# A linear-attention and GEGLU kernel on one core: the first v cast without Pool, one PSUM copy on ScalarE, and the last 128 output rows in three column parts

## The chip, the cores and the metric

One core of a Trainium2 chip. The metric is the device time of one execution in microseconds (us); smaller is better. A traced execution also has a span, from its first to its last instruction, some 1.8 us shorter than the time.

Engines in the profile: PE is TensorE's matmuls, PEld its weight loads, DVE is VectorE, ACT is ScalarE, POOL is GpSimd (Pool in the text), SP issues most transfers.

## The reference

```python
q_s = softmax over the last axis of q          # (8, 8, 576, 64)
k_s = softmax over the sequence axis of k
kv  = einsum('bhsd,bhse->bhde', k_s, v)
x   = einsum('bhsd,bhde->bhse', q_s, kv)       # transposed to (4608, 512)
out = (gelu(x @ w_gate) * (x @ w_val)) @ w_out # d_ff 1536, out (4608, 512) float32
```

## The kernel before

Everything runs in fp16 on TensorE. Per batch: exponentials of q and k, a cast of v, transposes of q (`unit_t`), the products of k and v (`unit_kv`), x transposed (`unit_x`), then the feed-forward stage (`ffn_fi`, 12 slices) and the output matmuls (`mm_out`), of which each row block of 128 ends in one PSUM bank and is evacuated (copied to SBUF) and stored by `evac`. Names in the profile: `eqt` is the transposed softmax of q, copied out of the PSUM tile `pst`; `pskv` holds the products of k and v, `kv_sb` what is kept of them; `xt` is x transposed, copied out of `psx`; `psg` and `psv` are the gate and value products, `ht` the input of the output matmuls. The parts that matter here (cut, `...` where lines are left out):

```python
ps_big = tile_pool(bufs=6, space=PSUM)     # six banks, tag "mm"
ps_att = tile_pool(bufs=2, space=PSUM)     # two banks, tag "att"

def unit_kv(b, g):
    pskv = ps_att.tile([P, 2, 2 * VW], f32, tag="att")
    # ... 2 x 5 matmuls, then VectorE: a reciprocal (rck) and two kv_sb ...

def unit_t(b, g, eng="dve"):
    pst = ps_att.tile([P, 2, MAIN], f16, tag="att")
    # ... 8 transposes ...
    copy_on(eng, eqt[:, 2 * g:2 * g + 2, 0:MAIN], pst)

# in evac, for the last row block of all (psy is one bank, hc = 256)
nc.vector.tensor_scalar(out=yo[:, 0:hc], in0=psy[:, 0:hc], ...)
store(nc.sync, yo[:, 0:hc], ns, ns + 1, 0, hc)
nc.scalar.activation(out=yb, in_=psy[:, hc:C], func=ACTF.Copy, ...)
store(nc.scalar, yb, ns, ns + 1, hc, C)

# the first batch, in program order
unit_t(0, 0, "dve")
warm_pe(6)                      # six matmuls that keep TensorE busy
cast_v(0, 0, 4, "dve")          # heads 0 to 3
cast_v(0, 4, 6, "act")
unit_t(0, 1, "dve")
cast_v(0, 6, 8, "pool")
unit_kv(0, 0); unit_kv(0, 1)
unit_x(0, 0, "act", True); unit_x(0, 1, "act", True)
cast_w("wg", 0, "pool"); cast_w("wv", 0, "pool")
unit_x(0, 2, "dve", True); unit_x(0, 3, "dve", True)
```

The softmax here doesn't subtract the row's maximum and nothing guards it: scores larger than these inputs give would overflow.

## Time and profile before

| | before |
|---|---|
| time, median of the first three runs | 329.2 us (329.01 to 329.72) |
| traced span | 327.7 us |
| PE busy | 317.5 us, 97% |
| first value matmul (all earlier work is ramp) | 18.88 us |
| last matmul's end to the end of the span | 323.53 to 327.7 us, 4.2 us |

How to read it: only where the chain of waits leaves PE can a microsecond be gained, which is at the two ends. The lines of the busy shares, of the chain and of both ends are in the prediction. One more pair of lines will matter, which I did not look at before predicting: the timeline of the kernel before near 73 us (start, duration in us, engine, line, operation, output<-inputs, shapes, count, and in brackets the idle time before it with its releaser).

```profile
73.18 0.82 DVE L167 TENSOR_TENSOR eq<-eq,rrq 128x640 f16<-128x640 f16 x1
73.22 2.69 POOL L119 CAST v<-vt 128x640 f16<-128x640 f32 x3 [10.70 <-PE psg L268]
```

VectorE's normalization (two SBUF inputs) starts 0.04 us ahead of Pool's v casts and takes 0.82 us.

### The profile page before, as it was taken

The numbers are of one execution on the slowest core, as the hardware profiler recorded it, in microseconds if no ns is written. First come the engines' busy times: TensorE is split into PE (matmuls) and PEld (weight loads), VectorE is DVE, ScalarE is ACT, GpSimd is POOL, SyncE is SP. The second block draws the span as 40 slices with busy tenths as digits, with TensorE's granted clock in tenths as the row PEclk, the third lists the DMA queues.
The fourth block names the chain that finished last, engine by engine and source line by source line (L and its number), as shares of the span: only waits on it lengthen the run. The fifth ranks groups of instructions, "written<-read, shape, count | busy, mean of one in ns | idle before, by whom it ended". The sixth has DMA issues, their size and how long they took to land.

```text
span 327.7 us, 4481 instructions
## 1 busy us (share of the span) xinstructions
PE 317.5 (97%) x1702; PEld 153.1 (47%) x1702; DVE 180.5 (55%) x327; ACT 146.0 (45%) x195; POOL 46.4 (14%) x59
## 2 busy tenths in 40 slices
PE   7699999999999999999999999999999999999994
PEld 2444454445454544554455445444544444444441
DVE  2753365497579636952597349733983233333331
ACT  3453574898344572349224922484243033103300
POOL 1576452303002100030004000300000000000000
PEclk9599999999999999999999999999999999999999
DMA  7999999960196016900590039202100110040002
GB/s 229 363 384 392 402 393 389 392 248 0 64 315 233 3 64 208 338 1 23 176 393 19 2 132 380 99 0 86 45 0 2 64 64 2 4 108 19 1 33 96
DMA packets 38358, 50.49 MB, mean 154 GB/s; under 512 B 2112, under 2 KB 34112, under 8 KB 38336
## 3 DMA queue, kind: packets, MB, share of 16 engines
q1 hardware_dynamic: 38192, 50.08, 42.9%
q8 instruction: 13, 0.21, 0.2%
q10 hardware_dynamic: 144, 0.13, 0.1%
q14 instruction: 9, 0.07, 0.1%
HBM read 40.76 MB, written 9.44 MB: 153 GB/s over the span
## 4 chain that ended last, share of the span: by engine, by line
PE 89%; DMA 5%; ACT 2%; DVE 2%; issue 1%; SPq 1%; POOL 0%; POOLq 0%; ACTq 0%
PE psy L312 28%; PE psv L268 26%; PE psg L268 26%; DMA kt<-in_k_dram 3%; PE pskv L194 3%; PE pst L219 2%; PE psx L246 2%; DMA qt<-in_q_dram 1%; PE pswarm L260 1%; SPq L103 1%; ACT xt L121 1%; DVE kv_sb L202 0%; PE pstr L231 0%; DVE rq L160 0%; ACT L143 0%
## 5 line engine op out<-in xcount | busy, mean ns | idle before, releaser
L273 ACT ACTIVATE gl<-psg 128x512 f32<-128x512 f32 x108 | 63.9, 598 | 137.9 <-PE psg L268 131.5
L275 DVE SCALAR_TENSOR_TENSOR ht<-psv,gl 128x512 f16<-128x512 f32 x108 | 73.9, 689 | 65.3 <-PE psv L268 63.2
L268 PE MATMUL psg<-xt,wg_sb 128*128 128x512 f16 x384 | 100.6, 379 | 0.7 <-ACT xt L121 0.5
L268 PE MATMUL psv<-xt,wv_sb 128*128 128x512 f16 x384 | 100.2, 379 | 0.1
L312 PE MATMUL psy<-wo_sb,ht 128*128 128x512 f16 x432 | 95.8, 379 | 0.0
L268 PEld LDWEIGHTS <-wv_sb 128*128 128x128 f16 x432 | 42.3, 98 | 51.8 <-issue 1.3
L312 PEld LDWEIGHTS <-ht 128*128 128x128 f16 x432 | 41.6, 98 | 48.5
L268 PEld LDWEIGHTS <-wg_sb 128*128 128x128 f16 x432 | 41.0, 98 | 44.8 <-issue 1.6
L346 DVE TENSOR_SCALAR yo<-psy 128x512 f32<-128x512 f32 x31 | 21.2, 687 | 49.2 <-PE psy L312 49.2
L119 POOL CAST v<-vt 128x640 f16<-128x640 f32 x26 | 20.6, 830 | 141.5 <-PE psx L246 64.3
L160 DVE TENSOR_REDUCE rq<-eq 128x10 f32<-128x640 f16 (+1 forms) x32 | 25.3, 791 | 10.2 <-ACT eq L143 10.2
L167 DVE TENSOR_TENSOR eq<-eq,rrq 128x640 f16<-128x640 f16 (+1 forms) x27 | 23.1, 856 | 0.9
L121 ACT CAST xt<-psx 128x512 f16<-128x512 f32 x26 | 14.5, 587 | 18.5 <-PE psx L246 18.5
L143 ACT ACTIVATE eq<-qt 128x2560 f16<-128x2560 f32 (+1 forms) x9 | 18.3, 2049 | 4.4 <-DMA qt<-in_q_dram 4.3
L143 ACT ACTIVATE ek<-kt 128x2048 f16<-128x2048 f32 (+1 forms) x10 | 15.6, 1558 | 4.2 <-DMA kt<-in_k_dram 4.2
L219 PE MATMUL pst<-ident,eq 128*128 128x128 f16 x128 | 10.7, 228 | 3.6 <-DVE eq L167 2.0
L219 PEld LDWEIGHTS <-eq 128*128 128x128 f16 x128 | 8.9, 102 | 7.9 <-ACT eq L143 2.5
L194 PEld LDWEIGHTS <-ek 128*128 128x128 f16 x160 | 11.0, 101 | 3.1
L268 PE MATMUL psg<-xtr,wg_sb 128*128 128x512 f16 x48 | 12.3, 379 | 0.0
L268 PE MATMUL psv<-xtr,wv_sb 128*128 128x512 f16 x48 | 12.3, 379 | 0.0
L194 PE MATMUL pskv<-v,ek 128*128 128x130 f16 x160 | 12.3, 227 | 0.0
L123 DVE COPY eqt<-pst 128x1024 f16<-128x1024 f16 x16 | 10.9, 679 | 0.6 <-PE pst L219 0.6
(52 smaller groups left out, 132.1 us busy)
## 6 DMA issues: line engine op xcount, KB each, us to landing
kt<-in_k_dram SPq DMA_DIRECT2D x14, 640.0 KB, 7.6
vt<-in_v_dram SPq DMA_DIRECT2D x14, 640.0 KB, 9.0
qt<-in_q_dram SPq DMA_DIRECT2D x14, 640.0 KB, 6.2
out_dram<-yo SPq DMA_DIRECT2D x14, 512.0 KB, 3.0
wost<-in_moe_w_out_dram SPq DMA_DIRECT2D x6, 512.0 KB, 8.8
wgst<-in_moe_w_gate_dram SPq DMA_DIRECT2D x5, 512.0 KB, 7.4
wvst<-in_moe_w_val_dram SPq DMA_DIRECT2D x5, 512.0 KB, 7.9
kt<-in_k_dram SPq DMA_DIRECT2D x4, 320.0 KB, 8.7
```

The costliest lines, as they stand in the source:

```text
L119: nc.gpsimd.tensor_copy(out=dst, in_=src)
L121: nc.scalar.copy(out=dst, in_=src)
L143: nc.scalar.activation(out=dst[:, c0:c1, h0 * D:h1 * D].rearrange("p n (h d) -> p h n d", d=D), in_=tiles[(nm, b)][:, h0:h1, c0 * D:c1 * D ...
L160: nc.vector.reduce_sum(rq, e, axis=mybir.AxisListType.X)
L167: (nc.gpsimd if eng == "pool" else nc.vector).tensor_tensor(out=e, in0=e, in1=rrq.unsqueeze(-1).to_broadcast((P, n, 2, D)), op=ALU.mult)
L194: nc.tensor.matmul(pskv[:, j, :], ek_b[b % 2][:, n, hp * P:(hp + 1) * P], v16_b[b % 2][:, n, 2 * hp:2 * hp + 2, 0:VW], start=(n == 0), sto ...
L219: nc.tensor.transpose(pst[:, j, n * P:(n + 1) * P], eq_b[b % 2][:, n + 1, hp * P:(hp + 1) * P], ident)
L268: nc.tensor.matmul(ps, w[:, ci, fi * P:(fi + 1) * P], xt[:, ci, :], start=(ci == 0), stop=(ci == HP - 1))
L273: nc.scalar.activation(out=gl, in_=psg, func=ACTF.Gelu)
L275: nc.vector.scalar_tensor_tensor(out=ht, in0=psv, scalar=_H_SCALE, in1=gl, op0=ALU.mult, op1=ALU.mult)
L312: nc.tensor.matmul(psy, hts[fi][:, ns * P:(ns + 1) * P], wo_sb[:, fi, :], start=(fi == 0), stop=(fi == NFI - 1))
L346: nc.vector.tensor_scalar(out=yo, in0=psy, scalar1=1.0 / _H_SCALE, scalar2=None, op0=ALU.mult)
```

## The change

Its intent at the start is to take Pool out of the first batch's v cast and a copy off VectorE; at the end, to have less work left when the last matmul ends.

```diff
-    htp = ctx.enter_context(tc.tile_pool(name="htp", bufs=14))
+    htp = ctx.enter_context(tc.tile_pool(name="htp", bufs=13))
...
+    def last_rows(b, hts, ns):
+        cuts = ((0, 256), (256, 384), (384, 512))
+        ps = [ps_big.tile([P, c1 - c0], f32, name="psl", tag="mm") for c0, c1 in cuts]
+        for part in ((0,), (1, 2)):
+            for fi in range(NFI):
+                for i in part:
+                    c0, c1 = cuts[i]
+                    nc.tensor.matmul(ps[i], hts[fi][:, ns * P:(ns + 1) * P], wo_sb[:, fi, c0:c1],
+                                     start=(fi == 0), stop=(fi == NFI - 1))
+            for i in part:
+                c0, c1 = cuts[i]
+                yl = yop.tile([P, c1 - c0], f32, name=f"yl{i}", tag=f"yl{i}", bufs=1)
+                if i < 2:
+                    nc.vector.tensor_scalar(out=yl, in0=ps[i], scalar1=1.0 / _H_SCALE,
+                                            scalar2=None, op0=ALU.mult)
+                else:
+                    nc.scalar.activation(out=yl, in_=ps[i], func=ACTF.Copy, scale=1.0 / _H_SCALE)
+                store(nc.scalar if i == 2 else nc.sync, yl, b, ns, ns + 1, c0, c1)
...   (the old two-halves code in evac goes; store is the same, moved out of evac)
-    unit_t(0, 1, "dve")
-    cast_v(0, 6, 8, "pool")
+    unit_t(0, 1, "act")
+    cast_v(0, 6, 8, "dve")
     unit_kv(0, 0)
     unit_kv(0, 1)
+    cast_w("wg", 0, "pool")
+    cast_w("wv", 0, "pool")
     unit_x(0, 0, "act", True)
     unit_x(0, 1, "act", True)
-    cast_w("wg", 0, "pool")
-    cast_w("wv", 0, "pool")
     unit_x(0, 2, "dve", True)
-    unit_x(0, 3, "dve", True)
+    unit_x(0, 3, "act", True)
```

More of the change, by code (lines that the diff above doesn't have):

```diff
@@ L313, in mm_out, with out_rows, store @@
                              start=(fi == 0), stop=(fi == NFI - 1))
+    def out_rows(b):
+        return out[b * S:(b + 1) * S, :].rearrange("(m n) c -> m n c", n=NT)
+    def store(eng, src, b, n0, n1, c0=0, c1=C):
+        base = out_rows(b)[:, 1 + n0:1 + n1, c0:c1]
+        (pm, nm), (pn, _), _ = base.ap
+        last = [[1, (n1 - n0) * C]] if c1 - c0 == C else [[1, c1 - c0]]
+        eng.dma_start(out=bass.AP(tensor=base.tensor, offset=base.offset,
+                                  ap=[[pm, nm], [NM * pn, 2]] + last), in_=src)
+    def last_rows(b, hts, ns):
[16 more added lines that the diff above has]
+                store(nc.scalar if i == 2 else nc.sync, yl, b, ns, ns + 1, c0, c1)
     def evac(b, ns, psy):
@@ L327, in evac @@
             return
-        rows = out[b * S:(b + 1) * S, :].rearrange("(m n) c -> m n c", n=NT)
-        def store(eng, src, n0, n1, c0=0, c1=C):
-            base = rows[:, 1 + n0:1 + n1, c0:c1]
-            (pm, nm), (pn, _), _ = base.ap
-            last = [[1, (n1 - n0) * C]] if c1 - c0 == C else [[1, c1 - c0]]
-            eng.dma_start(out=bass.AP(tensor=base.tensor, offset=base.offset,
-                                      ap=[[pm, nm], [NM * pn, 2]] + last), in_=src)
-        if b == order[-1] and ns == 3:
-            hc = C // 2
-            yb = yop.tile([P, hc], f32, name="yb", tag="yb", bufs=1)
-            nc.vector.tensor_scalar(out=yo[:, 0:hc], in0=psy[:, 0:hc], scalar1=1.0 / _H_SCALE,
-                                    scalar2=None, op0=ALU.mult)
-            store(nc.sync, yo[:, 0:hc], ns, ns + 1, 0, hc)
-            nc.scalar.activation(out=yb, in_=psy[:, hc:C], func=ACTF.Copy, scale=1.0 / _H_SCALE)
-            store(nc.scalar, yb, ns, ns + 1, hc, C)
-            return
         nc.vector.tensor_scalar(out=yo, in0=psy, scalar1=1.0 / _H_SCALE,
@@ L348, in evac @@
         if b == order[-1]:
-            store(nc.sync, yo, ns, ns + 1)
+            store(nc.sync, yo, b, ns, ns + 1)
         elif ns % 2 == 1:
-            store(nc.sync, yo_t[b].rearrange("p n c -> p (n c)"), ns - 1, ns + 1)
+            store(nc.sync, yo_t[b].rearrange("p n c -> p (n c)"), b, ns - 1, ns + 1)
     for src, nm, n0 in ((q, "q", 1), (k, "k", 0), (v, "v", 0)):
@@ L490 @@
             for ns in range(4):
+                if b == order[-1] and ns == 3:
+                    last_rows(b, hts, ns)
+                    break
                 psy = ps_big.tile([P, C], f32, name="psy", tag="mm")
```

## The prediction

> **What bounds the kernel now.** I read the page's busy shares first, then the chain that ended last, then that chain piece by piece over its first 40 us and its last 10 us, and last the timeline of each engine in those two stretches, since the change touches nothing between them. Before: 329.2 us (median of 329.01, 329.20 and 329.72); the traced span is 327.7 us.
>
> The page (busy share; then the chain's share by engine):
>
> ```profile
> PE 317.5 (97%) x1702; PEld 153.1 (47%) x1702; DVE 180.5 (55%) x327; ACT 146.0 (45%) x195; POOL 46.4 (14%) x59
> ...
> PE 89%; DMA 5%; ACT 2%; DVE 2%; issue 1%; SPq 1%; POOL 0%; POOLq 0%; ACTq 0%
> ```
>
> TensorE is the bound: the chain is 89% PE. A change can only pay where PE isn't the last link: some 20 us of ramp and about 4 us after the last matmul. The chain of waits through the ramp (start, us, what), where the change acts:
>
> ```profile
> 11.96 2.56 PE pswarm L260 x6
> 14.52 0.85 PE pst L219 x8
> 15.37 1.10 PE pskv L194 x10
> 16.47 0.02 issue
> 16.50 0.18 DVE rck L199
> 16.68 0.03 issue
> 16.70 0.61 DVE kv_sb L202 x2
> 17.31 0.09 DVE rck L199
> 17.40 0.02 issue
> 17.42 0.36 DVE kv_sb L202
> 17.79 0.05 issue
> 17.83 0.65 PE psx L246 x2
> ```
>
> The reader is to see that neither the v cast nor the evacuation of the second transposes (eqt) is a link here: PE runs warm-up, transposes and the first ten k-v matmuls without a gap, then VectorE's reciprocal waits for PE. The timeline of VectorE, and of the one Pool cast that goes away:
>
> ```profile
> 14.03 0.83 DVE L123 CAST v<-vt 128x1280 f16<-128x1280 f32 x1 [0.80 <-DMA vt<-in_v_dram]
> 14.05 1.38 POOL L119 CAST v<-vt 128x640 f16<-128x640 f32 x1 [0.19 <-DMA vt<-in_v_dram]
> ...
> 15.41 0.69 DVE L123 COPY eqt<-pst 128x1024 f16<-128x1024 f16 x1 [0.55 <-PE pst L219]
> ...
> 16.50 0.17 DVE L199 RECIPROCAL rck<-pskv 128x2 f32<-128x2 f32 x1 [0.39 <-PE pskv L194]
> ```
>
> VectorE is idle 0.39 us before the reciprocal, so taking the copy away from it frees nothing that the chain needs. The timeline of the end:
>
> ```profile
> 317.75 5.78 PE L312 MATMUL psy<-wo_sb,ht 128*128 128x512 f16 x26
> ...
> 323.56 0.42 DVE L340 TENSOR_SCALAR yo<-psy 128x256 f32<-128x256 f32 x1 [1.90 <-PE psy L312]
> 324.02 0.38 ACT L343 ACTIVATE yb<-psy 128x256 f32<-128x256 f32 x1 [11.08 <-DVE yo L340]
> 324.43 0.66 ACTq L334 DMA_DIRECT2D out_dram<-yb  x1
> ```
>
> PE ends at 323.53; the two halves of one bank are evacuated one after the other (ScalarE starts 0.04 us after VectorE ends), and the last store is issued at 324.43. The page of DMA issues gives it 2.2 us to land (326.63); about 1.07 us of the span follow.
>
> **What the Trainium skill says.** "PSUM — Partial Sum Buffer", section "PSUM bank collisions raise a hardware error": two engines must not access one bank and quadrant at once, even two readers at different addresses, so the compiler makes them wait for each other. The trace agrees: the releaser of ScalarE's half is VectorE's (line 324.02). Three banks remove that wait. "TensorE: Matmul & The Clock Gate", section "Wait — 56ns, not 53.3ns?": warm matmuls start N / 2.4 + 2.5 ns apart. The trace agrees: four 512-column matmuls take 0.86 us in the chain (0.216 each), ten of 130 columns 0.57 us (127.35 to 127.92, 57 ns each), eight of 128 columns 0.44 us (55 ns each), all with a weight load apiece; the same page's section "Back-to-back issue gap" has 81 ns for a real kernel at N = 128, which this trace doesn't show. Same page, "What's actually happening": the clock is half until a window of activity has passed, and the window is free-running; here the first ten k-v matmuls start 0.11 us apart and the last of the twenty about 0.06. "SBUF — State Buffer", section "SBUF: two separate sides": Pool and a VectorE operation in a two-port mode exclude each other for a whole instruction. The trace agrees: Pool's first v cast took 1.38 us against a median of 0.72 for 26 such casts, ending 0.57 after VectorE's.
>
> **The change, part by part: the start.** The order of instructions on PE is unchanged there.
>
> (a) Heads 6 and 7 of v move from Pool to VectorE. VectorE's 1280 elements took 0.83 us; half, with a fixed part of about 0.16 (estimate), is about 0.49 us, so it is done at 14.86 + 0.5 = 15.4, where Pool was done at 15.43. If Pool's first weight cast (its data land at 5.37 + 9.3 = 14.67) gets the shared port first, it is 15.9. These heads are first needed by the sixth matmul of the second group, after 16.5. Worth: 0.
>
> (b) Pool starts the weight casts without the v cast in front. The landings of the first four weight pieces (issue plus landing time) are 14.67, 15.52, 16.21 and 17.02, and the matmuls that need the first pair start at 18.3. In the before trace Pool ended these casts at 15.99, 16.55, 17.10 and 17.66. Worth: 0.
>
> (c) The second eqt evacuation moves to ScalarE, which is idle from 14.74 to 17.54. Its PSUM copies took 0.356 us for 256 columns and 0.587 for 512; at the same slope 1024 take about 1.05 (estimate), against 0.69 on VectorE. The end moves from 16.10 to about 16.44. That matters: the pool of attention banks has two buffers, so the second k-v group needs the bank that this copy releases. Before, its first weight load was at 16.22, which is 0.12 after the copy ended; now it is at about 16.56, and its first matmul slips from 16.25 to about 16.6. By then the clock is up in this trace (spacing 0.06 from about 16.5), so the tenth starts at 16.6 + 9 x 0.057 = 17.1 instead of 16.89: 0.2 later. The second reciprocal, which followed VectorE's first pair at 17.23, now waits for PE until about 17.35 to 17.4, and what follows it slips by 0.1 to 0.2. Half of that is absorbed: the second gate matmul waited for ScalarE's second xt (until about 18.61), not for PE. Cost: about 0.1 us, from 0 to 0.35.
>
> (d) The fourth xt moves from VectorE to ScalarE: done near 19.3 instead of 19.55, needed after 21.0; the gelu table load slips by 0.55 us to about 20.5, and the first gelu is at 21.45. Worth: 0.
>
> (e) Thirteen instead of fourteen ht buffers: twelve are live, the thirteenth takes the next stage's first tile, and its second is written after the last read of the tile that it replaces. Worth: 0.
>
> **The end.** PE: 12 matmuls of 256 columns at 0.109 = 1.31 us and 24 of 128 at 0.0557 = 1.34, together 2.65, instead of 12 x 0.2157 = 2.59: +0.06. As a 128-column matmul also leaves the pipe sooner (219 against 379 ns in the trace), the next-to-last one, which releases VectorE's quarter, ends where the old last one did, at 323.53; the very last at about 323.59. VectorE's quarter: 0.42 at 256 columns and 0.69 at 512 give about 0.29, done at 323.85. ScalarE's quarter beside it: about 0.28, done at 323.9 instead of 324.40. The last issue moves from 324.43 to about 323.93: -0.50. The first half's evacuation and store lie under the second half's matmuls. The two last stores, 64 KB each, now run at the same time, in rows of 512 B: before, 128 KB in rows of 1 KB moved in about 0.54 us after 1.3 us of issue and delay. I allow no gain and up to 0.1 us of loss for the shorter rows. Sum of the end: -0.50 + 0.05 = -0.45.
>
> **Sum**: -0.45 + 0.10 = -0.35 us on 329.2, or 328.85. As a shorter store can also land sooner (half the bytes, up to -0.2), I take 328.8.
>
> **The rivals.** First, the start loses more than the end gains: ScalarE's long copy delays the second k-v group, and if the clock comes up later than here (the window is free-running) the ten matmuls run at 0.11 and all 0.35 us stay: time 329.1 to 329.3. For it: the 0.12 us between the copy's end and the load, and only two buffers. Against it: the slack behind ScalarE's second xt. Second, the small matmuls cost more than their columns, 81 ns as the skill has it: 24 x 0.025 = 0.6 us more, which eats the end's gain: about 329.4. Against it: 55 and 57 ns in this trace. Third, the start gains because Pool no longer contends with VectorE for the port and the weights are ready earlier: up to 0.3 us, 328.5. Against it: neither is on the chain. Fourth, the stores end later because two small ones collide: +0.2, 329.0.
>
> **Range and chances.** Every term is below a microsecond, and 2% is 6.6 us, so within 2% is all but certain: 0.985, with 0.01 for faster and 0.005 for slower. The runs of before spread over 0.7 us, more than the effect; with the rivals, from 328.1 to 329.5.
>
> **What would show it.** The profile after should have the last ScalarE evacuation released by PE and overlapping VectorE's, the last issue 0.4 to 0.6 us nearer to 323.5 (counted with the start's shift), matmuls of 128 columns 55 to 57 ns apart, an eqt copy of about 1.0 us on ScalarE, and the second k-v group's load about 0.1 us after its end. It is wrong if that copy takes 0.7 us or less, if the first gate matmuls start earlier than 18.3, if the small matmuls are 80 ns apart, or if the last store takes over 2.5 us to land.

## The result and the profile after

The changed kernel took 328.82 us (median of 4 runs, 328.57 to 329.39) against 329.46 us (4 runs, 329.01 to 329.82) for the kernel before. The ratio is 0.9984, interval 0.9964 to 1.0004: the same within 2%. A ratio here is the mean time of one kernel's fast runs over that of the other's of the same rounds, so it is not quite the ratio of the medians. The prediction was 328.8.

Against differences of half a microsecond the runs spread by 0.8, so I read the traces stretch by stretch. The page after, the busy shares and the chain's shares by engine:

```profile
PE 317.9 (97%) x1726; PEld 154.5 (47%) x1726; DVE 180.6 (55%) x327; ACT 147.5 (45%) x197; POOL 45.1 (14%) x58
...
PE 90%; DVE 3%; ACT 2%; DMA 2%; issue 1%; POOL 0%; SPq 0%; DVEq 0%; ACTq 0%; POOLq 0%
```

PE has 24 more matmuls (1726 against 1702) and 0.4 us more busy time; the bound is the same. The chain of waits through the ramp, after:

```profile
15.51 1.08 PE pskv L194 x10
16.59 0.01 issue
16.61 0.89 PE pskv L194 x10
17.50 0.02 issue
17.52 0.18 DVE rck L199
17.70 0.02 issue
17.72 0.36 DVE kv_sb L202
18.09 0.05 issue
18.13 0.65 PE psx L246 x2
```

Where the chain before went from the first k-v group to VectorE's first reciprocal, it now goes through the second group on PE, which starts only at 16.61, and VectorE's second reciprocal (17.52) waits for it. What held it, in the timeline of ScalarE, and the weight loads from the group's second on:

```profile
15.54 1.01 ACT L121 COPY eqt<-pst 128x1024 f16<-128x1024 f16 x1 [0.53 <-PE pst L219]
...
16.61 0.69 PEld L194 LDWEIGHTS <-ek 128*128 128x128 f16 x9 [0.18 <-issue]
```

The copy ends at 16.55, and the second group's first matmul comes 0.06 us later, at 16.61; its weights had been loaded at 16.28 already, and the load shown, of the group's second matmul, comes at the same time. The clock was still at half when the group began: its first four matmuls start 0.06, 0.11 and 0.11 us apart, the last ones 0.06. The end, in the timeline after:

```profile
321.19 2.81 PE L333 MATMUL psl<-wo_sb,ht 128*128 128x256 f16 x36
...
323.99 0.29 DVE L339 TENSOR_SCALAR yl<-psl 128x128 f32<-128x128 f32 x1 [0.86 <-PE psl L333]
324.04 0.28 ACT L342 ACTIVATE yl<-psl 128x128 f32<-128x128 f32 x1 [10.69 <-PE psl L333]
324.35 0.66 ACTq L322 DMA_DIRECT2D out_dram<-yl  x1
```

ScalarE is released by PE, not by VectorE, and works beside it; both are done 0.32 us after PE's end at 324.00 (before: 0.87 us).

To compare traces I cut each in five:

- *lead*: up to the first transposes that Pool releases (11.35 us before); the landing of q sets it.
- *start*: from there to the first value matmul (psv).
- *A*: from there to the second batch's first k-v matmul.
- *B*: from there to VectorE's evacuation of the third row block of the last stage (its start is PE's progress).
- *end*: from there to the end of the span.

| | lead | start | A | B | end | normalization at 73 us | span |
|---|---|---|---|---|---|---|---|
| before | 11.35 | 7.53 | 29.86 | 272.23 | 6.73 | 0.82 | 327.70 |
| after | 11.48 | 7.59 | 29.87 | 272.45 | 6.18 | 1.35 | 327.57 |

All in us, differences of the starts in the timelines, rounded (0.01 us either way); the spans to two decimals are those of `prof LABEL --windows 0:`. The two spans differ by only -0.13: +0.13 + 0.06 + 0.01 + 0.22 - 0.55 = -0.13. So the end gave half a microsecond, the start cost 0.06, and in this one execution two things that I had not reckoned with took the rest: q landed 0.13 us later, and 0.22 us went in stretch B. There PE's starts, laid side by side, keep one distance from the first value matmul to 74 us and then slip by 0.22. The timeline after, there:

```profile
72.67 3.31 POOL L119 CAST v<-vt 128x640 f16<-128x640 f32 x4 [9.92 <-DMA vt<-in_v_dram]
...
73.38 1.35 DVE L167 TENSOR_TENSOR eq<-eq,rrq 128x640 f16<-128x640 f16 x1
```

This time Pool's casts came first, because v had landed sooner, and VectorE's normalization took 1.35 us in place of 0.82; the transposes of that data wait for it. Whether the change causes this, or chance, was to be tested.

### The profile page after: what moved, and what is told of

It reads as the page before. It is cut to its first block, busy times and chain, and to the rows that moved or that the text cites. A ratio compares the mean times of both kernels' runs of the same rounds, so it can differ in the third digit from the quotient of the medians.

```text
span 327.6 us, 4529 instructions
## 1 busy us (share of the span) xinstructions
PE 317.9 (97%) x1726; PEld 154.5 (47%) x1726; DVE 180.6 (55%) x327; ACT 147.5 (45%) x197; POOL 45.1 (14%) x58
## 4 chain that ended last, share of the span: by engine, by line
PE 90%; DVE 3%; ACT 2%; DMA 2%; issue 1%; POOL 0%; SPq 0%; DVEq 0%; ACTq 0%; POOLq 0%
PE psy L312 28%; PE psg L268 27%; PE psv L268 26%; PE pskv L194 3%; PE pst L219 2%; PE psx L246 2%; DMA qt<-in_q_dram 2%; DVE rq L160 1%; PE psl L333 1%; PE pswarm L260 1%; DVE eq L167 1%; DVE ht L275 1%; ACT eq L143 1%; PE pstr L231 1%; ACT L273 0%
## 5 line engine op out<-in xcount | busy, mean ns | idle before, releaser
L312 PE MATMUL psy<-wo_sb,ht 128*128 128x512 f16 x420 | 93.2, 379 | 0.0
L312 PEld LDWEIGHTS <-ht 128*128 128x128 f16 x420 | 40.5, 98 | 47.0 <-DVE ht L275 0.2
L119 POOL CAST v<-vt 128x640 f16<-128x640 f32 x25 | 19.0, 800 | 141.6 <-DMA vt<-in_v_dram 109.8
L121 ACT CAST xt<-psx 128x512 f16<-128x512 f32 x27 | 15.1, 588 | 17.1 <-PE psx L246 17.1
L143 ACT ACTIVATE ek<-kt 128x2048 f16<-128x2048 f32 (+1 forms) x10 | 15.6, 1559 | 4.1 <-DMA kt<-in_k_dram 4.1
L246 PE MATMUL psx<-eqt,kv_sb 128*128 128x512 f16 x32 | 10.7, 380 | 0.4 <-DVE kv_sb L202 0.2
```

The source lines that it names most:

```text
L119: nc.gpsimd.tensor_copy(out=dst, in_=src)
L143: nc.scalar.activation(out=dst[:, c0:c1, h0 * D:h1 * D].rearrange("p n (h d) -> p h n d", d=D), in_=tiles[(nm, b)][:, h0:h1, c0 * D:c1 * D ...
L246: nc.tensor.matmul(psx, st[(b, "kv", hp)].rearrange("p h e -> p (h e)"), st[(b, "eqt")][:, hp, 0:MAIN], start=True, stop=True)
L312: nc.tensor.matmul(psy, hts[fi][:, ns * P:(ns + 1) * P], wo_sb[:, fi, :], start=(fi == 0), stop=(fi == NFI - 1))
```

## The experiments

Theory: the end is worth about 0.5 us, the start costs about 0.1, and both can be read in the stretches. Rival 1: the start gains, by freeing Pool. Rival 2: the change brings the meeting at 73 us about. All kernels gave correct results. The stretches of every trace are in one table; each is one execution, the times are medians of several, the intervals are of 95%. By the granted clock of the traces, TensorE came to its full clock at 14.5 to 15.6 us in E1, E3, E5 and E9 to E12 (called early below), at 15.9 in E4, and at 16.3 to 17.1 in the first traces of before and after, E2, E6, E7 and E8 (late). In E4, E9 and E11 an earlier full stretch had lasted to 12.4, 11.8 and 12.1, so that their first warm-up matmuls before the k-v groups ran fast too.

| run | start | A | B | end | at 73 us | time (before) | ratio, interval |
|---|---|---|---|---|---|---|---|
| E1 end only | 6.94 | 29.87 | 272.46 | 6.19 | 1.37 | 328.86 (329.5) | 0.9985, 0.9972 to 0.9997 |
| E2 start only | 7.59 | 29.86 | 272.26 | 6.73 | 1.16 | 329.65 (329.5) | 1.0003, 0.9991 to 1.0015 |
| E3 copy on VectorE | 7.01 | 29.87 | 272.41 | 6.19 | 1.31 | 329.05 (329.5) | 0.9993, 0.9979 to 1.0006 |
| E4 own bank | 6.95 | 29.86 | 272.32 | 6.18 | 1.22 | 328.79 (329.5) | 0.9981, 0.9969 to 0.9993 |
| E5 two halves | 7.00 | 30.24 | 272.23 | 6.31 | 0.88 | 328.92 (329.55) | 0.9978, 0.9952 to 1.0004 |
| E6 shared bank | 7.51 | 29.87 | 272.41 | 6.30 | 1.30 | 329.26 (329.55) | 0.9987, 0.9961 to 1.0013 |
| E7 five warm-ups | 7.31 | 29.86 | 272.22 | 6.17 | 1.05 | 329.28 (329.55) | 0.9992, 0.9960 to 1.0024 |
| E8 four, split cast | 7.30 | 29.89 | 272.23 | 6.17 | 0.93 | 328.58 (329.55) | 0.9965, 0.9938 to 0.9993 |
| E9 changed, again | 7.04 | 29.87 | 272.22 | 6.18 | 0.87 | 328.87 (329.56) | 0.9975, 0.9952 to 0.9998 |
| E10 as E8, again | 6.40 | 30.48 | 272.24 | 6.18 | 1.06 | 328.58 (329.56) | 0.9971, 0.9944 to 0.9998 |
| E11 before, again | 7.02 | 29.87 | 272.23 | 6.73 | 0.83 | 329.27 | single run |
| E12 as E8, one cast moved | 6.54 | 29.86 | 272.23 | 6.18 | 0.92 | 328.74 (329.42) | 0.9978, 0.9939 to 1.0017 |

The kernel before had one run of 331.04 us in E5 to E10, which pulls those ratios down a little.

**E1, the end only** (the start as before, the rest as changed).

```diff
-    unit_t(0, 1, "act"); cast_v(0, 6, 8, "dve")      # and the order and engines after them
+    unit_t(0, 1, "dve"); cast_v(0, 6, 8, "pool")     # as in the kernel before
```

> Only the end of the change: three column parts with banks of their own, 13 ht buffers, the start as before. Theory (the end gains about 0.5 us, the start costs about 0.1): end stretch, from the start of VectorE's evacuation of the third row block to the end of the span, about 6.2 us as in the profile after, against 6.73 before; start stretch, from the first transposes that Pool releases to the first value matmul, about 7.53 as before; time 0.5 to 0.6 us under the kernel before (ratio near 0.9983). Rival (the gain comes from the start, Pool being freed): the end stretch near 6.7 and the ratio near 1.000.

The end stretch was 6.19 us and the ratio 0.9985: the theory's numbers, and not rival 1's. The expected start of 7.53 was missed: it was 6.94, with the same instructions as before. In this trace the first ten k-v matmuls ran from 15.07 to 15.81, where before they ran from 15.17 to 16.47: the clock had come up ahead of them. It also shows the bank wait without ScalarE: with the first group done early, the second waited 0.27 us, until after VectorE's copy of 0.69 us. Because of the clock a single trace's start can't be compared with another's unless both had it at the same time.

**E2, the start only** (the end and 14 ht buffers as before).

```diff
-    unit_t(0, 1, "dve"); cast_v(0, 6, 8, "pool")
+    unit_t(0, 1, "act"); cast_v(0, 6, 8, "dve")      # and the order and engines after them
```

> Only the start of the change: v cast by VectorE and ScalarE, the second eqt copy and the fourth xt on ScalarE, the end and 14 ht buffers as before. Theory: start stretch 7.55 to 7.75 us, as the eqt copy of 1.0 us holds the second k-v group back; end stretch 6.73 as before; time 0 to 0.3 us over the kernel before (ratio 1.000 to 1.001). Rival: start stretch under 7.4, ratio near 0.999.

Here the clock came up late, as in the first traces of before and after, and the start was 7.59: the changed kernel's number, 0.06 over the 7.53 of before. The end was 6.73. The time, 329.65, is not separable from before's 329.5. Rival 1 falls: the start's part gains nothing that these runs can tell. The 0.06 us is not the copy's alone: the clock was full at 16.84 here and at 16.94 in the trace after, but at 16.49 before (and at 16.33 in E6, which has the start of before and took 7.51). In the trace after, four steps between the group's matmuls of 0.06, 0.11, 0.11 and 0.09 us instead of 0.057 make some 0.14 us (an estimate from these spacings), about what the second reciprocal slipped, so what the copy itself costs with a late clock isn't separated.

**E3, the second transpose copy back on VectorE, behind both v casts.**

```diff
-    unit_t(0, 1, "act")
-    cast_v(0, 6, 8, "dve")
+    cast_v(0, 6, 8, "dve")
+    unit_t(0, 1, "dve")
```

> The changed kernel with only the second eqt copy given back to VectorE, behind both of its v casts. Theory: the copy takes 0.69 us instead of 1.01, the first weight load of the second k-v group comes about 0.3 us sooner against the start of the first group than in the profile after (1.05 us behind it instead of 1.36), start stretch near 7.5, end stretch near 6.2; time 0.05 to 0.2 under the changed kernel. Rival (VectorE was the bottleneck of the start and must be relieved): start stretch above 7.6, the first reciprocal later than 1.33 us behind the first k-v matmul.

The copy took 0.69 us, and the second group's first load came 1.07 us behind the first's, the expected number, but by coincidence: the clock was early, so the first group had needed only some 0.6 us and the second waited for the copy on VectorE too (0.30 us). The first reciprocal came 0.81 us behind the first k-v matmul, which is not the 1.33 of the rival. The start of 7.01 lies beside 7.04 of the changed kernel with an early clock (E9). The time didn't go below the changed kernel's (329.05, with two runs at 329.9), so what the copy's place is worth in time stays open; it is less than these runs can tell.

**E4, the second k-v group in a bank of the large pool.**

```diff
-    def unit_kv(b, g):
-        pskv = ps_att.tile([P, 2, 2 * VW], f32, name="pskv", tag="att")
+    def unit_kv(b, g, big=False):
+        pskv = (ps_big if big else ps_att).tile([P, 2, 2 * VW], f32, name="pskv",
+                                                tag="mm" if big else "att")
...
-    unit_kv(0, 1)
+    unit_kv(0, 1, True)
```

> The changed kernel, but the second k-v group of the first batch writes to a bank of the large pool, so that it no longer waits for the eqt copy on ScalarE. Theory: the group follows the first without a gap (first weight load about 1.05 us behind that of the first group instead of 1.36), although the copy still takes 1.0 us on ScalarE; start stretch 7.4 to 7.5; time 0.05 to 0.2 under the changed kernel. Rival (something else than the bank holds the group, such as the v cast of heads 6 and 7): the gap stays.

The timeline of weight loads and of ScalarE in this run:

```profile
14.71 1.01 ACT L121 COPY eqt<-pst 128x1024 f16<-128x1024 f16 x1 [0.27 <-PE pst L220]
14.81 1.62 PEld L195 LDWEIGHTS <-ek 128*128 128x128 f16 x20 [0.40 <-ACT v L121]
```

All twenty loads run on without a break. But this trace does not test the bank: the copy ended at 15.72 (14.71 + 1.01), and the second group's first load came at 15.77 and its first matmul at 15.87, after it. The transposes had been early here, so the group would hardly have had to wait in either bank. E7, with the same change and a late clock, is the test; its timeline:

```profile
15.00 2.26 PE L195 MATMUL pskv<-v,ek 128*128 128x130 f16 x20
15.19 1.01 ACT L121 COPY eqt<-pst 128x1024 f16<-128x1024 f16 x1 [0.45 <-PE pst L220]
```

There the second group's first matmul started at 16.04, 0.16 us before the copy's end at 16.20, with no gap among the twenty; in E10 and E12, also with a bank of its own, it was 0.40 and 0.43 us before. Without it, it came 0.05 to 0.06 us after ScalarE's copy in all three traces (after, E2, E9) and 0.15 us after VectorE's in all six (before, E1, E3, E5, E6, E11). So the bank is what held the second group. The rival, the cast of heads 6 and 7, did not in the trace after (it ended at 15.97, the group started at 16.61); it is the next wait once the bank's is gone and the clock is early: in E12 the group's sixth matmul came at 15.76, 0.30 us after its fifth, and that cast ended at 15.71. The start was 6.95, below the 7.4 to 7.5 that I expected, but the clock was up for a part of the warm-up matmuls here, so that gain isn't the bank's. The time, 328.79, is not separable from the changed kernel's.

**E5, two halves with a bank each; the second whole on ScalarE** (start as before).

```diff
-        cuts = ((0, 256), (256, 384), (384, 512))
+        cuts = ((0, 256), (256, 512))
-        for part in ((0,), (1, 2)):
+        for part in ((0,), (1,)):
```

> The start of the kernel before; the last row block in two halves of 256 columns with a bank each, computed one after the other, the first evacuated by VectorE under the second's matmuls, the second by ScalarE whole (0.38 us), stored in one piece of 128 KB. Theory (what pays is that only the last piece is left when PE ends, and that it is evacuated in one go): PE ends as before, ScalarE ends 0.42 us after it (0.87 before, 0.3 in the three parts), end stretch 6.3 us (6.73 before, about 6.2 after), ratio near 0.9987. Rival (the third bank matters most): end stretch near 6.5.

**E6, the second half in one bank, read by both engines** (start as before): as E5, but VectorE evacuates columns 256 to 383 and ScalarE 384 to 511 of the same bank.

```diff
-                yl = ...   # one piece, on ScalarE (both sides abridged)
+                for e0, e1, act in ((256, 384, False), (384, 512, True)):
+                    src = ps[i][:, e0 - c0:e1 - c0]   # VectorE, then ScalarE
```

> As the two halves, but the second half's bank is read by both engines, 128 columns each, in one bank: the pieces of the three-part end without the third bank. Theory (two readers of one bank take turns): ScalarE waits for VectorE's 0.29 us and then takes 0.28, so it ends 0.6 to 0.65 us after PE instead of 0.3, end stretch 6.45 to 6.55, ratio near 0.9993. Rival (the size of the pieces is what pays, the bank doesn't matter): both start together and the end stretch is 6.2.

The timeline of E5's ScalarE, then of E6's two evacuations:

```profile
323.53 0.39 ACT L342 ACTIVATE yl<-psl 128x256 f32<-128x256 f32 x1 [10.65 <-PE psl L333]
```

```profile
323.79 0.29 DVE L341 TENSOR_SCALAR yl<-psl 128x128 f32<-128x128 f32 x1 [0.89 <-PE psl L333]
324.11 0.28 ACT L344 ACTIVATE yl<-psl 128x128 f32<-128x128 f32 x1 [10.98 <-DVE yl L341]
```

In E6 the small pieces are there but ScalarE is released by VectorE again and ends 0.65 us after PE (PE ended at 323.74), as the theory has it; with banks of their own it was 0.32. So the bank is what makes them take turns, and the rival (size alone pays) is refuted. E5's single piece ended 0.44 us after PE and its end stretch was 6.31, as expected: 0.42 of the 0.55 us is already in having the first half under the second's matmuls and the second in one go; small pieces with a bank each add 0.12 to 0.14 us (from 6.31 to between 6.17 and 6.19). My figure for E6's end stretch, 6.45 to 6.55, was missed: it was 6.30, no longer than E5's. Up to the last issue E6 is slower, as the bank wait says: counted from the third row block's evacuation the last issue came at 3.46 us before, 3.26 in E6, 3.04 in E5 and 2.96 after. But from the last issue to the end of the span E6 took 3.04 us (327.46 - 324.42), where the changed kernel took 3.22 (327.57 - 324.35) and before 3.27 (327.70 - 324.43). There the last store of 64 KB ran after the other one and not beside it; that this is the cause is argued, not shown by a run of its own.

**E7 and E8, fewer warm-up matmuls, on top of E4.** E8 also casts heads 0 to 3 in two pieces, so that the first k-v matmuls can start after the first.

```diff
-    warm_pe(6)
-    cast_v(0, 0, 4, "dve")
+    warm_pe(4)                  # E7: warm_pe(5), and the cast in one piece
+    cast_v(0, 0, 2, "dve")
+    cast_v(0, 2, 4, "dve")
```

> The changed kernel with the second k-v group in a bank of the large pool, and five instead of six warm-up matmuls in front of the second transposes. Theory (PE, held by the warm-up matmuls at half clock, is what the first k-v group waits for, as the v cast is done some 0.3 us before it starts): with the clock still low the first k-v matmul starts 0.1 to 0.25 us after VectorE's first v cast ends instead of 0.3, start stretch 7.1 to 7.3 instead of 7.59; where the clock comes up before 15 us nothing changes (6.95). Ratio to the kernel before 0.997 to 0.9985. Rival (the warm-up matmuls bring the clock up, and one fewer brings it up later): start stretch 7.6 or more.

> As five warm-up matmuls, but four, and VectorE's v cast of heads 0 to 3 in two pieces of 640 elements, so that the first head pair's matmuls can start after the first piece. Theory: each piece takes about 0.5 us, the first k-v matmul starts 0.1 us after the first piece, about 0.3 us sooner than with five, start stretch 6.8 to 7.1, ratio 0.997 to 0.998. Rival (the clock comes up later, or the two casts cost more than they give): start stretch 7.3 or more.

E7: the first k-v matmul came at 15.00, 0.14 us after VectorE's cast ended (14.03 + 0.83), and the start was 7.31 against 7.59 with a late clock. The start is shorter by 0.28, as expected, though how much of that is due to E4's bank and how much to the warm-up matmul isn't separated; the timed runs (329.28) don't show it, with an interval that holds both. E8: v landed late in the traced run (VectorE's cast began at 14.44, 14.31 in the trace after and 14.03 in E7), and the first k-v matmul came at 15.08; so its start was only 7.30, above the expected 6.8 to 7.1. Its runs were the fastest, 0.9965.

**E9, E10 and E11, the changed kernel, E8's and the kernel before once more**, for second traces, the first two beside each other.

> The changed kernel once more, for a second trace and beside the next run on the same chip. Theory: end stretch 6.15 to 6.21 again; start stretch 7.59 if the clock comes up near 16.5 us, 6.95 to 7.1 if before 15; middle (first value matmul to the evacuation of the third row block) 302.1 plus 0 to 0.24 for the meeting of Pool's v cast with VectorE's normalization at 73 us, which is chance; ratio 0.998 to 0.9988. Rival (the change itself brings that meeting about): middle again 302.3.

> Four warm-up matmuls, the v cast in two pieces and the k-v group's own bank, with the three-part end, once more: ratio 0.9965 to 0.9978, 0.2 to 0.5 us under the changed kernel beside it; start stretch 6.8 to 7.3, depending on when v lands. Rival (the 0.9965 was a lucky draw of the clock and nothing but the end counts): ratio 0.9983, as the changed kernel.

> The kernel before once more, for a second trace. Theory: end stretch 6.70 to 6.75; start stretch 7.5 or, with an early clock, 6.95; the normalization at 73 us takes between 0.82 and 1.37 us by chance, not always 0.82. Rival (the kernel before avoids that meeting by its order): 0.82 again.

E9 and E11 both had an early clock, and the starts were 7.04 and 7.02; the ends 6.18 and 6.73. So with an early clock the changed start costs 0.02 us here, or 0.04 to 0.10 against E5 and E1, which have the start of before (v landed at different times in all of them), and the end gains 0.55. (E9's ratio, 0.9975, fell just below the expected 0.998 to 0.9988.) E9's normalization at 73 us took 0.87 us, so the changed kernel can do without the loss. It is set by when v lands against VectorE's turn, and E2, with the old end, had it at 1.16. But my expectation for E11, a time between 0.82 and 1.37, not always 0.82, was not borne out: it was 0.83, its rival's number. In both traces of the kernel before, Pool's first cast came after VectorE's normalization (by 0.05 and 0.23 us), in all twelve others 0.2 to 1.0 us ahead of it. Rival 2 is therefore weakened and not refuted: that the change makes the meeting likelier stays open, and with it up to 0.23 us of stretch B. E1 and E2, with one half of the change each, both have it, so no single part explains it. Over all traces B is 272.22 to 272.26 where the normalization took 1.16 us or less, and 272.32 to 272.46 where it took 1.22 or more.

E10 was a surprise. Its start was 6.40, 0.64 below E9's, but A was 30.48 in place of 29.87: at the second batch the gain was gone. The timeline of E10:

```profile
42.48 1.04 POOL L119 CAST wo_sb<-wost 128x1024 f16<-128x1024 f32 x1 [0.24 <-DMA wost<-in_moe_w_out_dram]
42.76 1.43 DVE L167 TENSOR_TENSOR eq<-eq,rrq 128x640 f16<-128x640 f16 x1
...
46.70 0.40 PE L220 MATMUL pst<-ident,eq 128*128 128x128 f16 x4 [0.51 <-POOL eq L167]
```

PE is now so early that VectorE's first normalization for the second batch falls into a Pool cast of output weights, which starts when its data land. It takes 1.43 us; Pool's own normalization, behind VectorE's sums, comes late, and the transposes wait 0.51 us. E5 shows the same in small (A 30.24, a wait of 0.27).

**E12, that cast on ScalarE**, which is idle then.

```diff
-    at(0, FI, NFI - 1, L(exp, "q", 1), L(exp, "k", 1, 0, 4),
-       L(cast_w_o, 3), L(cast_w_o, 4), L(cast_w_o, 5),
+    at(0, FI, NFI - 1, L(exp, "q", 1), L(cast_w_o, 5, "act"), L(exp, "k", 1, 0, 4),
+       L(cast_w_o, 3), L(cast_w_o, 4),
```

> Four warm-up matmuls, the v cast in two pieces, the k-v group's own bank and the three-part end, and besides the last of the six casts of the output weights, near 42.5 us, on ScalarE (idle there for 1.5 to 2.5 us) instead of Pool. Theory (what the shorter start gained was given back at 43 us, where this Pool cast held VectorE's first normalization of the second batch to 1.43 us instead of 0.82, so that the second transposes waited 0.51 us for Pool): the normalization takes 0.82 to 0.83 us, no wait of the transposes for Pool, 29.87 us from the first value matmul to the second batch's first k-v matmul instead of 30.48, start stretch 6.4 to 7.3; ratio 0.9950 to 0.9965, time 327.8 to 328.4. Rival (the second batch's loads set that point anyway): the 30.5 us stay and the ratio is 0.997.

```profile
42.08 1.04 ACT L121 CAST wo_sb<-wost 128x1024 f16<-128x1024 f32 x1 [0.21 <-DMA wost<-in_moe_w_out_dram]
43.00 0.83 DVE L167 TENSOR_TENSOR eq<-eq,rrq 128x640 f16<-128x640 f16 x1
```

The normalization is back at 0.83 us, no transposes wait, A is 29.86, and the start of 6.54 is kept: the span of 326.3 us is the shortest traced, 0.3 under E9's and E10's 326.6. So the meeting of that Pool cast with VectorE's normalization was the cause of the loss in A, and the rival (the loads) is refuted, as far as one trace of each shows. The timed runs don't confirm a gain: this ran on a chip where the kernel before spread from 328.49 to 332.56 us and this one from 328.06 to 330.23, and the ratio, 0.9978 (0.9950 to 0.9965 expected), has an interval from 0.9939 to 1.0017. E8's kernel, with 328.58, is the best by time, 0.3 us under the changed kernel beside it, but their intervals overlap. No version is shown to beat the changed kernel.

## Why the prediction was right

It was right in the time (328.8 predicted, 328.82 measured) and in where it comes from, the end. The agreement to 0.02 us is luck: the runs spread by 0.8 us, the predicted drop of 0.4 us was counted from a median of three runs, 329.2, where later calls gave 329.42 to 329.56, and the end gained more than reckoned (0.55 for 0.45). Its terms can be checked one by one.

- **The end's evacuations, -0.50.** Counted from the start of the third block's evacuation, the last issue came at 324.43 - 320.97 = 3.46 us before and at 324.35 - 321.39 = 2.96 after: -0.50. ScalarE was released by PE, the quarters took 0.29 and 0.28 us as extrapolated. E6 shows that the separate bank is what lets them overlap, E5 that most of the gain needs no third bank, only an early first half and the second in one piece.
- **The small matmuls, +0.06 on PE.** The 36 matmuls took 2.66 us in the chain; 2.65 was reckoned. Less 12 x 0.109 us for the wide ones, which is the prediction's figure, 24 take 1.35, or 56 ns each. The rival of 81 ns falls.
- **The stores, +0.05: sign wrong, size small.** The prediction allowed a loss for rows of 512 B. The two stores landed 1.9 and 2.1 us after their issue, before 2.1 and 2.2, and from the last issue to the end of the span it was 3.22 instead of 3.27 us; the end as a whole shortened by 0.54 to 0.56 in every trace with three parts, not 0.45.
- **The start, (a) and (b), 0.** VectorE's two casts took 1.66 us together in the trace after, where Pool's first weight cast (15.01, 0.61 us) came between them; in E3 VectorE went first, its casts took 1.23 together and Pool's 0.94. In the trace after they were done at 15.97, before heads 6 and 7 were needed. Pool's first four weight casts ended at 15.62, 16.44, 17.20 and 17.92; the last is later than before because everything landed later in that run.
- **The start, (c), +0.10: the wait right, the size in part by luck.** The copy took 1.01 us (1.05 reckoned), and the bank carried the wait (E7, E10 and E12 against after, E2 and E9). The group's first matmul followed the copy by 0.06 us, where 0.16 was reckoned (16.6 against 16.44); but the clock, reckoned to be up from 16.5, was full only at 16.81 (16.94 less the 0.13 of the lead). The two misses cancel: the group's last matmul started at 17.13 (17.26 less 0.13) against the 17.1 reckoned. The start was 0.06 us longer with a late clock, of which the clock's own part isn't separated, and 0.02 to 0.10 with an early one. The half of the slip that the slack was to take was rather two thirds: the second reciprocal slipped by 0.16 us (17.52 against 17.23, less the 0.13 of the lead), and the first value matmul by 0.06.
- **(d) and (e), 0.** The fourth xt ended at 19.40 and the gelu table at 20.70, both in time. With 13 and with 14 buffers B is the same where the normalization took 1.06 us or less (272.22 to 272.24 with 13 in E5, E7 to E10 and E12; 272.23 with 14 in the traces of before).

The prediction had the wrong view of one thing, the noise: it knew that the clock's window runs freely but took its effect for the difference between two versions' terms (0 to 0.35 us). In fact it moves the whole start from 7.5 to 7.0 us in either version, and meetings of Pool and VectorE move stretch B by up to 0.24 us. A trace pair alone (327.7 and 327.6) would have shown almost nothing of the 0.5 us.

## What to carry to other kernels

When the last matmul ends, what is left should be small and should not share a PSUM bank: compute the first part of the last block early (0.42 us here), and give each engine that evacuates the rest its own bank (0.12 to 0.14 more). Look for the wait behind a moved copy: here a copy that was off the chain held a bank that the next matmuls needed. Where one execution is noisier than the effect, cut traces into stretches between fixed instructions and compare those; and expect an earlier start to change what meets what later on, since a gain of 0.6 us at 18 us was lost at 43 us to two engines wanting one port.

## What the Trainium skill lacked or had wrong

- "TensorE: Matmul & The Clock Gate", section "Back-to-back issue gap", gives about 81 ns as the sustained spacing of matmuls with weight loads at N = 128. Here 24 of them, each with its own load, took about 56 ns each, the figure that the page calls the isolated gap (its sustained figure for N = 512 is about 131 ns, where 512-column matmuls here took 216).
- "TensorE: Matmul & The Clock Gate", section "What's actually happening", says that the transition to the full clock varies by 500 ns either way with the phase of the window, but not what that does to a short start. Here it came at 16.49 and 15.56 us in two traces of the kernel before and at 16.74 and 14.91 in two of E8's kernel, 1.8 us apart, and the start of the kernel before took 7.53 and 7.02 us, a difference as large as the effect under study.
- "SBUF — State Buffer", section "SBUF: two separate sides", has the lock between Pool and VectorE right (a normalization with two SBUF inputs took 0.82 us alone and up to 1.43 behind a Pool cast), but says nothing of how a start that gets shorter can move such a pair onto each other: 0.51 us of waiting transposes in E10, none in E12.
